# Seven block products in the experts' second layer as well, on a planned order of all engines, in a kernel of clustered attention and eight experts

## The chip, the cores and the metric

The kernel runs on one core of a Trainium2 chip. The metric is the device time of one execution in microseconds (us). TensorE is called PE here, VectorE DVE, ScalarE ACT, GpSimd POOL, and SyncE, which issues all DMAs, SP. "PEld" is the loading of a matmul's stationary operand.

## The reference, cut to what matters

```python
# attention: q, k, v are [4, 8, 768, 64]; a query sees the keys of its own cluster
scores = np.where(mask, scale * q @ k.T, -1e9); attn = softmax(scores); y = attn @ v
x = y.transpose(0, 2, 1, 3).reshape(3072, 512)
# experts: w_gate [512, 8], w1 [8, 512, 1024], w2 [8, 1024, 512]
P = exp(x @ w_gate - max)
for _ in range(8):                      # rows, then columns
    P /= P.sum(1, keepdims=True) + 1e-9; P /= P.sum(0, keepdims=True) + 1e-9; P *= N / E
for e in range(8):
    h = np.maximum(x @ w1[e], 0.0)      # first layer
    out += P[:, e:e + 1] * (h @ w2[e])  # second layer
```

All is float32.

## The kernel before, in words

**Attention.** The first stage works through 16 pairs of heads. A planner (`Planner`) sets its order: each step is a generator that yields an engine with a planned cost, and the planner records the instructions in the order of a planned time; `keep_order` makes each engine keep it. The result is x transposed, per batch of 768 tokens, stored in DRAM as `xd[b]`. `scan_first` finds expert 0's largest weights there, `first_x` makes the first batch's input tiles.

**Experts, first layer.** A number is held as two float16 parts, high and low, and a product is three matmuls: high by high, high by low, low by high. The tokens of a batch are split in two halves of 384, the 512 inputs in two halves, the features of a pair of 128-blocks in two: a 2x2 by 2x2 block product in seven products instead of eight (`layer1`). The seven operands from x (`XS`, with `LESS` for their differences) are made once per batch, the seven from the weights once per pair (`make_w`: four sums, then high and low parts). Each of the seven products is 6 matmuls (`product`, L1171), 128x128 stationary by 384 columns. Between them ACT scales a result out of PSUM (`scaled`, L1198) or DVE adds one (`add`, L1193); `relu_split` makes the high part with ReLU on ACT (L1182) and the low part on DVE (L1183). PSUM `h_ps` has two buffers.

**Experts, second layer.** It is a plain product (`layer2`): for each of 6 token blocks 6 matmuls of 512 columns (L1233 to L1235), summed in six PSUM banks over the four pairs of feature blocks. Once per batch and expert DVE takes the six results out, with the gate as factor, into `acc` (L1251, L1253).

I call one batch, one expert and one pair of feature blocks a **block**: 42 matmuls of 384 columns and 36 of 512. There are 4 x 8 x 4 = 128 blocks. Batches 0 and 1 take turns by expert through all eight experts, then batches 2 and 3.

**Weights.** In batch 0's turns `make_w` makes each pair's tiles `wa` (first layer) and `wb` (second layer, only split in high and low) and SP stores them in `wd`; every other batch loads them (`load_w`, 96 times). `scan` finds the next experts' largest weights. `gates` makes P, its 8 rounds crossing from DVE to PE and back.

**Order.** In this stage the code itself sets the order: the loop over `order` steps through generators (`making`, `scanning`, `inputs`, `sink`) between the seven products; layer 2 of a block runs between the products of the next one.

## Time and profile before

| What | Value |
|---|---|
| time, median of 3 runs | 2500.53 us (2497.03 to 2503.77) |
| profiled execution: span | 2493.7 us |
| its time around the span | not recorded apart; the median stands 6.8 us above the span |
| PE busy | 2390.6 us (96%), 12848 matmuls |
| DVE busy | 1372.4 us (55%) |
| ACT busy | 829.5 us (33%) |
| POOL busy | 669.5 us (27%) |
| first matmul of the first layer | 531.96 us after the span's start |
| last attention work on PE | 542.4 us |
| batches 2 and 3 | from about 1560 us to the end |

A row of a group reads: line, engine, operation, output<-inputs, shapes, count, then busy us, mean ns of one, then the engine's idle time just before them and what ended it. A row of a timeline reads: start us, duration us, engine, line, operation, count, and in brackets idle time and its releaser. A row of windows reads: stretch, its length, then busy us and count of PE, PEld, DVE, ACT and POOL, the granted share of the PE clock, the DMA engines' share and GB/s.

### The profile page before, as it was taken

The page shows a single profiled execution, that of the slowest core. Times are in us where ns is not written, and L with a number is a line of the kernel's source. Part 1 is how long each engine was busy: PE and PEld are TensorE (multiplying, and loading weights), DVE is VectorE, ACT ScalarE, POOL GpSimd, SP SyncE. Part 2 cuts the span into 40 slices and gives each one's busy share as a digit, 9 for nine tenths or more (in the row PEclk, how much of TensorE's full clock was granted, in tenths as well). Part 3 has the DMA queues.
Part 4 walks back from the last instruction along what each step waited for, and adds up shares of the span by engine and source line. Part 5 has one row for each costly group of instructions (what it writes and reads, how often), then busy time and mean ns, then how long its engine had stood idle before and what let it go on. Part 6 is the DMA issues. An engine that isn't in the chain of part 4 may idle for free.

```text
span 2493.7 us, 32865 instructions
## 1 busy us (share of the span) xinstructions
PE 2390.6 (96%) x12848; PEld 1281.1 (51%) x12848; DVE 1372.4 (55%) x2395; ACT 829.5 (33%) x1565; POOL 669.5 (27%) x683
## 2 busy tenths in 40 slices
...
DVE  7888787858755544444444446544443444444443
...
GB/s 165 139 120 121 124 99 112 97 144 232 237 277 255 147 158 108 146 124 130 135 141 113 125 47 138 103 113 96 93 101 108 94 94 109 101 93 94 114 103 89
DMA packets 154683, 320.30 MB, mean 128 GB/s; under 512 B 61088, under 2 KB 90528, under 8 KB 154016
## 3 DMA queue, kind: packets, MB, share of 16 engines
...
## 4 chain that ended last, share of the span: by engine, by line
PE 70%; DVE 8%; POOL 7%; DMA 7%; issue 6%; ACT 2%; SPq 0%; POOLq 0%; ACTq 0%; DVEq 0%
PE h_ps L1171 26%; PE o_ps L1233 10%; PE o_ps L1234 10%; PE o_ps L1235 10%; PE av_ps L817 4%; DMA r<-in_moe_w 3%; DMA scan<-in_moe_w 2%; POOL r L1091 2%; PE exp_ps L758 2%; PE max_ps L690 2%; PE exp_ps L759 2%; DVE mrt L694 2%; POOL wb L1100 1%; POOL wa L1103 1%; DVE am L286 1%
## 5 line engine op out<-in xcount | busy, mean ns | idle before, releaser
L1171 PEld LDWEIGHTS <-wa 128*128 128x128 f16 x5376 | 526.8, 98 | 478.5 <-issue 53.2
L1183 DVE SCALAR_TENSOR_TENSOR hl<-c,hh 128x384 f16<-128x384 f32 x512 | 313.6, 613 | 543.2 <-ACT hh L1182 542.7
L1171 PE MATMUL h_ps<-xsT,wa 128*128 128x384 f16 x3072 | 585.0, 327 | 13.8 <-ACT c L1198 6.9
L1233 PE MATMUL o_ps<-wb,hh 128*128 128x512 f16 x1536 | 584.5, 381 | 0.3 <-ACT hh L1182 0.3
L1234 PE MATMUL o_ps<-wb,hh 128*128 128x512 f16 x1536 | 583.9, 380 | 0.0
L1235 PE MATMUL o_ps<-wb,hl 128*128 128x512 f16 x1536 | 583.3, 380 | 0.7 <-DVE hl L1183 0.6
L1182 ACT ACTIVATE hh<-c 128x384 f16<-128x384 f32 x512 | 266.8, 521 | 853.4 <-DVE c L1193 848.5
L1171 PE MATMUL h_ps<-xsB,wa 128*128 128x384 f16 x2304 | 424.0, 328 | 25.1 <-DVE c L1193 20.9
L784 POOL TENSOR_TENSOR psum<-psum,pe 128x512 f32<-128x512 f32 (+1 forms) x216 | 231.4, 1088 | 57.3 <-ACT pe L765 50.1
L1235 PEld LDWEIGHTS <-hl 128*128 128x128 f16 x1536 | 151.0, 98 | 181.7 <-DVE hl L1183 2.9
L1193 DVE SCALAR_TENSOR_TENSOR c<-h_ps,u 128x384 f32<-128x384 f32 x256 | 142.0, 555 | 179.0 <-PE h_ps L1171 177.5
L1193 DVE SCALAR_TENSOR_TENSOR u<-h_ps,m 128x384 f32<-128x384 f32 x256 | 141.9, 554 | 163.7 <-PE h_ps L1171 163.7
L1233 PEld LDWEIGHTS <-hh 128*128 128x128 f16 x1536 | 150.8, 98 | 141.2 <-issue 1.7
L1234 PEld LDWEIGHTS <-hh 128*128 128x128 f16 x1536 | 150.7, 98 | 140.1 <-issue 1.6
L694 DVE TENSOR_REDUCE mrt<-max_ps 128x1 f32<-128x512 f32 (+1 forms) x288 | 190.5, 682 | 26.3 <-PE max_ps L690 24.1
L765 ACT ACTIVATE pe<-exp_ps 128x512 f32<-128x512 f32 x288 | 167.1, 597 | 111.4 <-PE exp_ps L759 96.2
L1198 ACT ACTIVATE c<-h_ps 128x384 f32<-128x384 f32 x128 | 62.5, 488 | 406.5 <-PE h_ps L1171 406.5
L1095 POOL TENSOR_TENSOR wa<-r,wa 128x256 f16<-128x256 f32 (+1 forms) x62 | 59.2, 972 | 344.6 <-ACT wa L1094 344.6
L1253 DVE SCALAR_TENSOR_TENSOR acc<-o_ps,gates,acc 128x512 f32<-128x512 f32 x168 | 125.3, 746 | 43.8 <-PE o_ps L1235 43.8
L690 PE MATMUL max_ps<-kX,qX 96*128 96x256 f32 (+1 forms) x384 | 127.2, 393 | 12.5 <-DVE mrt L694 11.7
L817 PE MATMUL av_ps<-pe,vn 128*64 128x512 f32 (+1 forms) x768 | 137.6, 501 | 0.0
L1091 POOL TENSOR_TENSOR r<-r 128x256 f32<-128x256 f32 x124 | 98.4, 814 | 116.1 <-ACT r L1081 113.7
...
## 6 DMA issues: line engine op xcount, KB each, us to landing
...
```

Source lines behind the costliest of these rows:

```text
L690: nc.tensor.matmul(ps[:, y * (z - a) : (y + 1) * (z - a)], t["qa"][0:96, i * P : (i + 1) * P], t["k2"][0:96, a:z], start=True, stop=True)
L694: nc.vector.tensor_reduce(out=t["mr"][:, i0 : i0 + ni, ni - 1], in_=ps.rearrange("p (x c) -> p x c", x=ni), axis=AX, op=ALU.max)
L765: nc.scalar.activation(pe, ps.rearrange("p (x c) -> p x c", x=ni), AF.Exp, scale=SCALE)
L784: (nc.gpsimd if e == POOL else nc.vector).tensor_tensor(out=st[:, a:z], in0=old[a], in1=part, op=ALU.add)
L817: nc.tensor.matmul(av[o, a:z], vn[:, i, :], heads[t]["pe", c][:, i - i0], start=(i == 0), stop=False, skip_group_check=True)
L1171: nc.tensor.matmul(ps[:, 0:HB], wa[:, w_, a, c, :], x[:, x_, c, :], start=(first and s_ == 0), stop=(s_ == len(steps) - 1), skip_group_che ...
L1182: nc.scalar.activation(hh[:, 2 - i, o], src, AF.Relu)
L1183: nc.vector.scalar_tensor_tensor(out=hl[:, 2 - i, o], in0=src, scalar=0.0, in1=hh[:, 2 - i, o], op0=ALU.max, op1=ALU.subtract)
L1193: nc.vector.scalar_tensor_tensor(out=t, in0=ps[:, 0:HB], scalar=KAPPA, in1=x, op0=ALU.mult, op1=ALU.add)
L1233: nc.tensor.matmul(po[i], hh[:, t, ti], wbh[:, t], start=(first and t == 0), stop=False)
L1234: nc.tensor.matmul(po[i], hh[:, t, ti], wbl[:, t], start=False, stop=False)
L1235: nc.tensor.matmul(po[i], hl[:, t, ti], wbh[:, t], start=False, stop=(last and t == 1))
```

## The change

**Second layer.** It is done in seven products too. Here the 2x2 blocks are the two token halves, the two feature blocks of a pair, and two halves of 256 output columns. The sums of h are made after ReLU on DVE (`relu_with`) and split like h itself (`split_raw`, `split_sum`); the sums of the weights are made once (`make_second`), split, and kept in DRAM (`wd2`). A **unit** is now one batch, one expert and two pairs of feature blocks: 84 matmuls of 384 columns and 7 x 3 x 6 = 126 of 256 columns. There are 64 units. `PIECES` lists the seven products, each in a part of two token blocks and a part of one. Their sums run in three PSUM banks (`a`, `c` and `ac`, which holds the third token block of both), and after each part DVE adds the running sum to `acc` with the gate (`collect`): 21 times per unit, 256 columns each. `BEFORE` says which `collect` a part waits for.

**First layer.** The same seven products in another order (`STEPS`), running through two `a` buffers and one `b` and one `c`; ACT scales four results out, DVE adds three.

**Order.** The whole stage is recorded by a second `Planner`; PE's order is written out in `run_pe` (one product of layer 1, then one part of layer 2 of the unit 18 products before), and the work of DVE, POOL, ACT and SP is put around it by planned costs. Sums and low parts go to POOL or DVE, as `either` chooses.

**Weights and batches.** From expert 1 on, batches 0 and 1 use a weight tile in turn before it is given up, so a tile is made or loaded once for the two; batches 2 and 3 do it from expert 0 (64 loads instead of 192). Expert 1 is scanned in the attention stage too. For batches 0 and 1, expert 0 is collected without a gate, and ACT applies the gate later.

```diff
-    LESS = {"T2": (("T1", "B12", "B11"), ("T2", "B22", "T1")), "B21": (("T4", "B21", "T2"), ("T3", "B22", "B12"))}
+    LESS = {
+        "T1": (("T1", "B12", "B11", "B11"), ("T3", "B22", "B12", "B12")),
+        "T2": (("T2", "B22", "T1", "T1"),),
+        "T4": (("T4", "B21", "T2", "B21"),),
+    }
...
-        def scan_first():
-            am8 = sm.tile([P, 2, NF], F32, name="am8", bufs=1)
+        def scan_first(e):
+            am8 = sm.tile([P, 2, NF], F32, name="am8")
...
+        for e in range(2):
+            plan.spawn(scan_first(e), urgency("values", nheads - 12 + 4 * e))
...
-    hp = ctx.enter_context(tc.tile_pool(name="hp", bufs=2))
-    ps_h = ctx.enter_context(tc.tile_pool(name="ps_h", bufs=2, space=PSUM))
-    ps_o = ctx.enter_context(tc.tile_pool(name="ps_o", bufs=6, space=PSUM))
...
+    rawp = ctx.enter_context(tc.tile_pool(name="rawp", bufs=4, **tiled))
+    sump = ctx.enter_context(tc.tile_pool(name="sump", bufs=2, **tiled))
+    cp = ctx.enter_context(tc.tile_pool(name="cp", bufs=2, **tiled))
+    wap = ctx.enter_context(tc.tile_pool(name="wap", bufs=4, **tiled))
+    NH = 20
+    hp = ctx.enter_context(tc.tile_pool(name="hp", bufs=NH, **tiled))
+    wbp = ctx.enter_context(tc.tile_pool(name="wbp", bufs=4, **tiled))
+    xp = ctx.enter_context(tc.tile_pool(name="xp", bufs=1, **tiled))
+    accp = ctx.enter_context(tc.tile_pool(name="accp", bufs=1, **tiled))
+    gs = ctx.enter_context(tc.tile_pool(name="gs", bufs=2, **tiled))
+    ps_a = ctx.enter_context(tc.tile_pool(name="ps_a", bufs=2, space=PSUM, **tiled))
+    ps_b = ctx.enter_context(tc.tile_pool(name="ps_b", bufs=1, space=PSUM, **tiled))
+    ps_c = ctx.enter_context(tc.tile_pool(name="ps_c", bufs=1, space=PSUM, **tiled))
+    ps_g = ctx.enter_context(tc.tile_pool(name="ps_g", bufs=1, space=PSUM, **tiled))
+    ps_2 = ctx.enter_context(tc.tile_pool(name="ps_2", bufs=1, space=PSUM, **tiled))
...
+    units = []
+    for c in range(B // 2):
+        for e in range(E):
+            turns = [(j, g) for g in range(NG2) for j in range(2)] if e else [(j, g) for j in range(2) for g in range(NG2)]
+            units += [(2 * c + j, e, g) for j, g in turns]
+    NU = len(units)
+    uses = {}
+    for u, (b, e, g) in enumerate(units):
+        uses.setdefault((b // 2, e, g), []).append(u)
...
+    ONE, TWO = 0.975, 0.982
+    SLOT = 14 * (ONE + TWO)
...
+    plan.PATIENCE = {"PE": 0.0, "ACT": 0.1, "POOL": 0.1, "SP": 0.1, "DVE": 0.1}
+    plan.free.update({PE: LEAD, ACT: 0.0, DVE: 0.0, POOL: 0.0, SP: 0.0})
...
+    def make_second(e, f2):
+
+        idx = e * NP2 + f2
+        s = uses[0, e, f2 // 2][0] + 1
+        need = piece_time(s, f2 % 2)
+        yield from after(s - 3)
+        yield ev["scale", e]
+        yield t_wb
+        yield t_raw
...
+        for o, a, b_, op in ((0, (0, 1), (0, 0), ALU.subtract), (1, None, (1, 1), ALU.subtract), (2, (1, 1), (0, 1), ALU.subtract), (3, (1, 0), None, ALU.add)):
+            w = yield either(0.82, 0.4)
...
+            by(w).tensor_tensor(out=T_[:, o], in0=x, in1=y, op=op)
...
+        t = wb[0, e, f2] = wbp.tile([P, 2, 7, MH], F16, name="wb")
+        for o, a, cost in ((slice(0, 1), Bk[:, 0, 0:1], 0.4), (slice(1, 3), Bk[:, 1], 0.61), (slice(3, 7), T_, 1.04)):
+            if cost > 0.4:
+                yield ACT, cost
+            nc.scalar.copy(t[:, 0, o], a)
+            w = yield either(2 * cost, 1.15 * cost)
+            by(w).tensor_tensor(out=t[:, 1, o], in0=a, in1=t[:, 0, o], op=ALU.subtract)
...
+        nc.sync.dma_start(out=wd2[idx], in_=t.rearrange("p x a m -> p (x a m)"))
...
+    STEPS = ((A11, "B11", "a"), (S1, "T1", "c"), (S2, "T2", "a"), (S4, "B22", "c"), (S3, "T3", "a"), (A12, "B21", "b"), (A22, "T4", "a"))
...
+        yield (t_a, t_c, ev["m1", k], ev["m5", k], ev["u2", k], t_b, ev["c22", k])[n]
+        yield PE, ONE
...
+    def scaled(t, ps, func=AF.Copy):
+        nc.scalar.activation(t, ps[:, 0:HB], func, scale=KAPPA)
+
+    def plus(t, ps):
+        nc.vector.scalar_tensor_tensor(out=t, in0=ps[:, 0:HB], scalar=KAPPA, in1=t, op0=ALU.mult, op1=ALU.add)
...
+    def split_raw(k, o, c):
+        yield t_h
+        yield ACT, 0.522
+        t = h[k, o] = hp.tile([P, 2, HB], F16, name="h")
+        nc.scalar.activation(t[:, 0], c, AF.Relu)
+        yield DVE, 0.607
+        nc.vector.scalar_tensor_tensor(out=t[:, 1], in0=c, scalar=0.0, in1=t[:, 0], op0=ALU.max, op1=ALU.subtract)
...
+    def split_sum(k, o, c):
+        yield t_h
+        yield ACT, 0.522
+        t = h[k, o] = hp.tile([P, 2, HB], F16, name="h")
+        nc.scalar.copy(t[:, 0], c)
+        w = yield either(0.95, 0.54)
+        by(w).tensor_tensor(out=t[:, 1], in0=c, in1=t[:, 0], op=ALU.subtract)
...
+            nc.vector.scalar_tensor_tensor(out=out_, in0=c, scalar=0.0, in1=other, op0=ALU.max, op1=op)
...
+        relu_with(s_1, c11, h21, ALU.add)
+        relu_with(h21, c22, h21, ALU.subtract)
+        relu_with(c22, c22, s_1, ALU.subtract)
+        relu_with(c12, c12, c22, ALU.add)
...
+    PIECES = (("A12", 1, "c", (1, 1)), ("A11", 0, "a", (1, 1)), ("S1", 3, "c", (2, 2)), ("S2", 4, "a", (1, 2)), ("S3", 5, "a", (2, 2)), ("A22", 6, "a", (2, 1)), ("S4", 2, "c", (1, 2)))
...
+    BEFORE = {
+        (0, 0): ((1, 6, 0),), (0, 1): ((1, 6, 1), (1, 5, 1)),
+        (1, 0): ((1, 5, 0),), (1, 1): ((0, 0, 1), (1, 5, 1)),
+        (2, 0): ((0, 0, 0),), (2, 1): ((0, 1, 1), (0, 0, 1)),
+        (3, 0): ((0, 1, 0),), (3, 1): ((0, 2, 1), (0, 1, 1)),
+        (4, 0): ((0, 3, 0),), (4, 1): ((0, 3, 1),),
+        (5, 0): ((0, 4, 0),), (5, 1): ((0, 4, 1),),
+        (6, 0): ((0, 2, 0),), (6, 1): ((0, 5, 1), (0, 2, 1)),
+    }
+    COLS = ((0, 1), (2,))
...
+        for d, m_, half_ in BEFORE[m, half]:
+            if u >= d:
+                yield ev["v", u - d, m_, half_]
+        yield PE, TWO * (4 if half == 0 else 2) / 3
+        opens = m in (0, 1) or (m == 2 and half == 0)
+        fresh = m < 3
+        for i in COLS[half]:
+            n = 0
+            for j in range(2):
+                t, w = h[(u, j), o], wb[b // 2, e, 2 * g + j]
+                for a_, b_ in ((0, 0), (0, 1), (1, 0)):
+                    nc.tensor.matmul(
+                        view(m, i), t[:, a_, i * P : (i + 1) * P], w[:, b_, x, :],
+                        start=(opens and n == 0 and i in (0, 2)), stop=(n == 5), skip_group_check=True,
+                    )
+                    n += 1
...
+            yield DVE, 0.37
...
+            if plain and first:
+                nc.vector.tensor_copy(to, src)
+            elif plain:
+                nc.vector.tensor_tensor(out=to, in0=src, in1=to, op=ALU.add)
...
+                nc.vector.scalar_tensor_tensor(
+                    out=to, in0=src, scalar=gate[b, e][:, ti : ti + 1], in1=to, op0=ALU.mult, op1=ALU.add
+                )
...
+    def run_pe():
+        ones_ = [(u, j, n) for u in range(NU) for j in range(2) for n in range(7)]
+        twos = [(u, m, half) for u in range(NU) for m in range(7) for half in range(2)]
+        for i in range(len(ones_) + 14 + LAG):
+            if i < len(ones_):
+                u, j, n = ones_[i]
+                if j == n == 0:
+                    ev["slot", u].set(plan)
+                yield from layer1(u, j, n)
+            if i >= 14 + LAG:
+                yield from layer2(*twos[i - 14 - LAG])
```

The first place is PE at the end of attention. Before, with `misc_ps` and `av_ps` of the last pair of heads and `h_ps` of the first layer:

```order
L817 MATMUL av_ps<-pe,vn 64x512 x4
L817 MATMUL av_ps<-pe,vn 64x256 x4
L825 MATMUL av_ps<-nht_206,ve 128x512
L825 MATMUL av_ps<-nht_206,ve 128x256
L854 MATMUL misc_ps<-psum,ones 32x384 x4
L1171 LDWEIGHTS wa
L1171 MATMUL h_ps<-xsB_5493,wa 128x384
```

In the changed kernel (`g_ps` is of the gates, `a_ps` of the first layer):

```order
L858 MATMUL misc_ps<-psum,ones 32x384 x4
L869 MATMUL misc_ps<-ident,sc 128x128 x3
L892 MATMUL misc_ps<-ident_r,rr 24x128
L903 MATMUL misc_ps<-rt,spread 128x128 x6
L934 MATMUL misc_ps<-xT,wg 32x256 x12
L946 MATMUL misc_ps<-ident,gt 128x96 x2
L1064 MATMUL g_ps<-ident,gmax 1x128
L1331 LDWEIGHTS wa
L1331 MATMUL a_ps<-xsB_5577,wa 128x384
```

The first layer stood between the steps of the last pair; now it stands behind all of them and behind the gates' first transpose.

The second place is POOL at the same point. Before, once the last sums of attention (`psum`) are done, it makes the next two pairs' weights, since DVE has made the first (`r` is the raw weight and its sums):

```order
L1091 TENSOR_TENSOR r_6163<-r_6163 128x256 x4
L1091 TENSOR_TENSOR r_6138<-r_6138 128x256 x3
L1095 TENSOR_TENSOR wa<-r_6138,wa 128x256
L1091 TENSOR_TENSOR r_6138<-r_6138 128x256
L1095 TENSOR_TENSOR wa<-r_6138,wa 128x512
L1103 TENSOR_TENSOR wa<-r_6138,wa 128x1024
L1100 TENSOR_TENSOR wb<-r_6140,wb 128x1024
L1095 TENSOR_TENSOR wa<-r_6163,wa 128x256
L1095 TENSOR_TENSOR wa<-r_6163,wa 128x512
L1100 TENSOR_TENSOR wb<-r_6165,wb 128x1024
L1103 TENSOR_TENSOR wa<-r_6163,wa 128x1024
```

In the changed kernel the first of all the sums stand between the last `psum` (`raw` and `sums` are the weights and their sums, `wa` and `wb` the low parts):

```order
L788 TENSOR_TENSOR psum<-psum,pe 128x256
L1162 TENSOR_TENSOR sums<-sums,raw 128x256
L788 TENSOR_TENSOR psum<-psum,pe 128x256
L1162 TENSOR_TENSOR sums<-raw 128x256
L788 TENSOR_TENSOR psum<-psum,pe 128x256
L1162 TENSOR_TENSOR sums<-raw 128x256
L1162 TENSOR_TENSOR sums<-sums,raw 128x256
L1170 TENSOR_TENSOR wa<-raw,wa 128x256
L1162 TENSOR_TENSOR sums<-raw,sums 128x256
L1170 TENSOR_TENSOR wa<-raw,wa 128x512
L1170 TENSOR_TENSOR wa<-sums,wa 128x1024
L1205 TENSOR_TENSOR sums<-raw 128x256
```

POOL now makes most of the first weights of both layers, beginning inside the tail of attention.

The third place is DVE in the middle of batches 0 and 1. Before (`u`, `c` are first-layer results, `hl` the low parts):

```order
L1193 SCALAR_TENSOR_TENSOR u_13341<-h_ps,m_13325 128x384
L1183 SCALAR_TENSOR_TENSOR hl<-c_13359,hh 128x384
L1193 SCALAR_TENSOR_TENSOR u_13379<-h_ps,m_13325 128x384
L1193 SCALAR_TENSOR_TENSOR c_13395<-h_ps,u_13379 128x384
L1183 SCALAR_TENSOR_TENSOR hl<-c_13395,hh 128x384
L1193 SCALAR_TENSOR_TENSOR c_13413<-h_ps,m_13325 128x384
L1183 SCALAR_TENSOR_TENSOR hl<-c_13413,hh 128x384
L1193 SCALAR_TENSOR_TENSOR c_13431<-h_ps,u_13341 128x384
L1183 SCALAR_TENSOR_TENSOR hl<-c_13431,hh 128x384
L1253 SCALAR_TENSOR_TENSOR acc_6827<-o_ps,gates,acc_6827 128x512
L1193 SCALAR_TENSOR_TENSOR u_13464<-h_ps,m_13448 128x384
```

In the changed kernel (`c`, `s`, `h_` numbers are results and sums of one pair, `h` the split parts, `acc` the collected sums):

```order
L1354 SCALAR_TENSOR_TENSOR c_11976<-b_ps,c_11976 128x384
L1558 SCALAR_TENSOR_TENSOR acc_7453<-ac_ps,gates,acc_7453 128x256
L1162 TENSOR_TENSOR sums<-raw 128x256
L1445 SCALAR_TENSOR_TENSOR s_12135<-c_11976,h_12129 128x384
L1558 SCALAR_TENSOR_TENSOR acc_7453<-a_ps,gates,acc_7453 128x256
L1362 SCALAR_TENSOR_TENSOR h<-c_11976,h 128x384
L1558 SCALAR_TENSOR_TENSOR acc_7453<-a_ps,gates,acc_7453 128x256
L1558 SCALAR_TENSOR_TENSOR acc_7453<-ac_ps,gates,acc_7453 128x256
L1445 SCALAR_TENSOR_TENSOR h_12129<-c_12000,h_12129 128x384
L286 TENSOR_REDUCE am_11240<-raw 128x1
L1445 SCALAR_TENSOR_TENSOR c_12000<-c_12000,s_12135 128x384
L1558 SCALAR_TENSOR_TENSOR acc_7559<-c_ps,gates,acc_7559 128x256
```

Collects of the second layer now stand between nearly all other instructions of DVE, with scans and weight sums among them.

659 lines of the change are left out of this document (401 added, 258 removed).

## The prediction

> **What bounds the kernel now.** I read the page first, then windows by stage, then timelines of the places that the change touches.
>
> ```profile
> span 2493.7 us, 32865 instructions
> PE 2390.6 (96%) x12848; PEld 1281.1 (51%) x12848; DVE 1372.4 (55%) x2395; ACT 829.5 (33%) x1565; POOL 669.5 (27%) x683
> DVE  7888787858755544444444446544443444444443
> ```
>
> PE is busy nearly throughout, but the share is a mean. (The third line is DVE's busy tenths in 40 slices; attention takes the first nine.) By stage (columns as in the note on windows above):
>
> ```profile
> 543.60:620.00 76.40, 57.06 (x259) 27.87 (x259) 59.63 (x127) 27.97 (x43) 30.61 (x25) 0.87 0.66 241
> 620.00:860.00 240.00, 218.38 (x1144) 111.73 (x1142) 154.34 (x241) 86.71 (x143) 81.20 (x72) 0.99 0.66 235
> 860.00:1560.00 700.00, 685.39 (x3645) 356.15 (x3644) 324.04 (x556) 233.24 (x401) 190.29 (x158) 1.00 0.36 124
> 1560.00:2494.00 934.00, 928.75 (x4959) 484.95 (x4956) 394.88 (x696) 192.97 (x386) 4.87 (x2) 1.00 0.28 100
> 1800.00:1900.00 100.00, 100.00 (x537) 52.29 (x536) 38.75 (x69) 20.72 (x42) 0.00 (x0) 1.00 0.27 95
> ```
>
> In batches 2 and 3 (from 1560) PE never rests: 537 matmuls in 100 us, so a block of 78 takes 14.5 us. In batches 0 and 1 it idles 19 us at the start, 22 up to 860, 15 after. DVE has half its time free, POOL three quarters or all. So the experts' stage is PE-bound; what the change does to PE's work counts in full, what it gives DVE and POOL counts once they fill up.
>
> ```profile
> 1700.01 1.14 PE L1171 MATMUL h_ps<-xsT,wa 128*128 128x384 f16 x6
> 1700.99 0.38 PE L1233 MATMUL o_ps<-wb,hh 128*128 128x512 f16 x1
> 1701.20 0.38 PE L1234 MATMUL o_ps<-wb,hh 128*128 128x512 f16 x1
> 1701.21 0.10 PEld L1235 LDWEIGHTS <-hl 128*128 128x128 f16 x1
> 1701.42 0.38 PE L1235 MATMUL o_ps<-wb,hl 128*128 128x512 f16 x1
> 66.00 0.34 PE L621 MATMUL misc_ps<-ident_b,om 128*128 128x128 bf16 x3
> ```
>
> A matmul's price is the distance of starts, not its duration. Six of 384 columns take 0.98 us, 0.1625 each; one of 512 takes 0.215.
>
> **PE's work.** Layer 1 keeps its 128 x 42 = 5376 matmuls: 5376 x 0.1625 = 873.6 us. Layer 2 had 4608 of 512 columns, 4608 x 0.2155 = 993.0 us. Now it has 64 x 126 = 8064 of 256 columns. No such row exists. Half of 0.2155 is 0.108; the line through 384 and 512 columns gives 0.2155 - 2 x 0.053 = 0.110. I take 0.109: 879 us, and 1753 us for both layers against 1867. The gain is **114 us**. It needs each matmul's own weight load (0.10 us) to fit under 0.109. That is close, but L621 issues three with a load each in 0.34 us, 0.06 apart after the first one's 0.22, so loads don't have to stand 0.10 apart. I charge nothing.
>
> **Where the stage begins.**
>
> ```profile
> 531.96 0.99 PE L1171 MATMUL h_ps<-xsB,wa 128*128 128x384 f16 x5
> 543.04 0.27 PE L1022 MATMUL h_ps<-ident,gmax 128*1 128x128 f32 x1 [0.69 <-DVE gmax L1019]
> 543.68 1.14 PE L1171 MATMUL h_ps<-xsT,wa 128*128 128x384 f16 x6 [0.37 <-DVE g L1024]
> 2488.89 0.38 PE L1235 MATMUL o_ps<-wb,hl 128*128 128x512 f16 x1
> ```
>
> Before, layer 1 fills gaps of attention's tail from 531.96. In the new order it stands behind L1064, the old L1022, so it starts at about **543.6**. In attention itself 16 more scans (half the width of L286 below, 0.6 us) lie on a DVE that has a fifth of its time free; I charge 0, at most 5.
>
> **The start-up.**
>
> ```profile
> L1091 POOL TENSOR_TENSOR r<-r 128x256 f32<-128x256 f32 x124 | 98.4, 814 | 116.1 <-ACT r L1081 113.7
> L1100 POOL TENSOR_TENSOR wb<-r,wb 128x1024 f16<-128x1024 f32 x31 | 66.7, 2152 | 128.0 <-ACT wb L1099 128.0
> L1095 POOL TENSOR_TENSOR wa<-r,wa 128x512 f16<-128x512 f32 x31 | 36.0, 1163 | 1.6 <-ACT wa L1094 1.6
> L1095 POOL TENSOR_TENSOR wa<-r,wa 128x256 f16<-128x256 f32 x31 | 24.2, 782 | 343.0 <-ACT wa L1094 343.0
> L296 POOL TENSOR_TENSOR tx<-xqB,tx 128x768 f32<-128x768 f32 x6 | 12.4, 2072 | 127.2 <-DVE xsT L303 63.7 <-issue 49.3 <-DMA xqB<-xd 14.1
> ```
>
> Up to the second `wb`, which layer 2 of the first unit needs, POOL's queue holds 16 sums (0.81), 3 + 4 + 5 low parts of 256, 512 and 1024 columns (0.78, 1.16, 2.15), 3 input sums (2.07), a split (384 columns, between the L1095 rows: 0.97) and three `psum`: about 41 us. It starts them near 531, so `wb` is there at 572 or, with waits for DVE, 576. PE is through the 18 products ahead of layer 2 at 543.6 + 18 x 0.975 = 561: 15 us of waiting. The fourth `wa` comes 15 us later still; I add 8 for it and 5 for the gates' crossings, which stand in PE's order: **28 us** (10 to 45).
>
> **DVE in batches 0 and 1.** This is the term I know least.
>
> ```profile
> L1193 DVE SCALAR_TENSOR_TENSOR c<-h_ps,u 128x384 f32<-128x384 f32 x256 | 142.0, 555 | 179.0 <-PE h_ps L1171 177.5
> L1253 DVE SCALAR_TENSOR_TENSOR acc<-o_ps,gates,acc 128x512 f32<-128x512 f32 x168 | 125.3, 746 | 43.8 <-PE o_ps L1235 43.8
> L904 DVE TENSOR_TENSOR xT<-misc_ps,xT 128x512 f32<-128x512 f32 x16 | 10.9, 684 | 9.7 <-PE misc_ps L899 9.6
> L904 DVE TENSOR_TENSOR xT<-misc_ps,xT 128x256 f32<-128x256 f32 x16 | 6.7, 417 | 4.8 <-PE misc_ps L899 4.7
> L286 DVE TENSOR_REDUCE am<-scan 128x1 f32<-128x1024 f32 x56 | 67.8, 1211 | 27.0 <-DMA scan<-in_moe_w 26.8
> L1183 DVE SCALAR_TENSOR_TENSOR hl<-c,hh 128x384 f16<-128x384 f32 x512 | 313.6, 613 | 543.2 <-ACT hh L1182 542.7
> L1183 DVE SCALAR_TENSOR_TENSOR hl<-c,hh x512: 495/558/1967, 539.7 to 2482.7; 128x384 f16<-128x384 f32 x171
> 2482.68 0.56 DVE L1183 SCALAR_TENSOR_TENSOR hl<-c,hh 128x384 f16<-128x384 f32 x1 [0.59 <-ACT hh L1182]
> 2483.16 0.74 DVE L1253 SCALAR_TENSOR_TENSOR acc<-o_ps,gates,acc 128x512 f32<-128x512 f32 x1
> ```
>
> A collect of 256 columns is L1253 less the difference of the two L904 rows: 0.746 - 0.267 = 0.48 us. Per unit: 21 x 0.48 = 10.1; 6 additions x 0.555 = 3.3; 6 low parts and 8 sums, x 0.558 = 7.8; 2 scans x 1.21 = 2.4; some 3 weight sums and splits 1.5; scales and gates 1: **26.1 us**. Two instructions that wait for nothing overlap: L1253 starts 0.48 after a start that lasts 0.56. Fifty overlaps of 0.08 make it 22.0. PE needs 84 x 0.1625 + 126 x 0.109 = 27.4 us per unit. So DVE just fits, were it alone. It isn't:
>
> ```profile
> 869.43 0.63 DVE L1183 SCALAR_TENSOR_TENSOR hl<-c,hh 128x384 f16<-128x384 f32 x1 [0.59 <-ACT hh L1182]
> 870.61 2.13 POOL L1100 TENSOR_TENSOR wb<-r,wb 128x1024 f16<-128x1024 f32 x1
> 871.62 1.54 DVE L1183 SCALAR_TENSOR_TENSOR hl<-c,hh 128x384 f16<-128x384 f32 x1 [1.09 <-ACT hh L1182]
> ```
>
> The second L1183 lasts 0.98 longer; it ends 0.42 after POOL's instruction does. DVE instructions with both inputs in SBUF stretch beside a busy POOL; L1193, which reads PSUM, doesn't. The new DVE has some 15.4 such of 384 columns per unit (6 + 8 + 1.4 splits). POOL's share per unit: 6.6 splits x 0.97, 6.2 sums x 0.81, 2 x 2.15, 1.6 x 1.16, 1.8 x 0.78 = 19 us, two thirds of the time. Lower bound of the stretch: L1183's mean over all is 0.613, 0.055 above its median, all from the half of them in batches 0 and 1, where POOL was busy a third: 0.11 each, 0.22 at two thirds, 3.4 us per unit. Upper: 0.98 x 2/3 x 15.4 = 10 us. I take the mean of the two rows above, (0.07 + 0.98) / 2 x 2/3 x 15.4 = 5.3, and for the bare work the middle, 24.1, as about half of the instructions follow a fresh result of ACT or PE. DVE then needs **29.5 us** per unit (25.4 to 36), 2.1 more than PE; over the 28 units after the start-up 28 x 2.1 = **59 us** (0 to 240).
>
> The Trainium skill says in "SBUF — State Buffer", Who interferes with whom, that a DVE instruction with two SBUF inputs contends with GpSimd's reads for one port pair held as an exclusive lock, the loser blocked for the whole instruction. By that, each such instruction waits on the mean 0.58 us whenever POOL is in one (the rest of instructions of the lengths above), 15.4 x 2/3 x 0.58 = 6.0 us per unit instead of 5.3, and the sum would be 20 us higher, an estimate. The row at 871.62 agrees with the lock.
>
> **The rest.** Batches 2 and 3: DVE has no scans and no weights, 21.7 us by durations, 18 overlapped; POOL makes 7 splits, 6.5 us, so 2 us of stretch. It fits under 27.4. What is late there is a collect: between a part and the next one that needs its bank PE has two products and a part of one block, 0.975 x 2 + 0.65 = 2.6 us, and two collects take 0.9, so DVE may be 1.7 late. I add 15 (before: 5 us idle there; 0 to 60). At the change of batches the inputs of batch 2 and then 3 put 14 us on DVE within one unit each: 2 x 7 = 15. ACT goes from 233 / 700 x 29.2 = 9.7 us per two blocks, by ten more instructions of 0.5 and the new weight sums' parts, to some 16.5 of 27.4: covered. DMAs halve in batches 2 and 3. Behind PE's last matmul come 4.8 us as before and about 1 of waits: 6.
>
> **Sum.** 543.6 + 1753 + 28 + 59 + 15 + 15 + 6 = 2420 us of span. The median stands 6.8 above the profiled span: 2427, 2.9% faster.
>
> **The rivals.** *DVE keeps up in batches 0 and 1 too* (T = 27.4 per unit): half of POOL's work falls where DVE reads PSUM. Without the 59 and some of the start-up: 2360. For it speaks the lower bound, 25.4; against it that DVE's order is fixed, so its idle moments aren't used. *DVE and POOL hold each other* in batches 0 and 1: at 33 us per unit (the full durations, 26.1, and 6.9 of stretch) the loss is 28 x 5.6 = 157 instead of 59, 2525, slower. It decides from 32 us per unit on (73 more over 28 units). By the Trainium skill's lock, as above, full durations would give 32.1, an estimate. Against it: the POOL row at 870.61 is not longer than its mean. *Collects come too late in all 64 units*: parts wait for banks throughout; 0.1 us on each of the 896 parts costs 75 more after what is charged, 2502, the same as before. *Loads don't hide under 256 columns*: at 0.12 per matmul 89 us more, 2516; L621 speaks against it.
>
> **Chances.** Forecast (DVE a little over PE in batches 0 and 1) 0.50; DVE keeps up 0.20; DVE and POOL hold each other 0.17, half of it slower; late collects 0.09, a third slower; loads 0.04. Faster than 0.3%, which is about what a measurement tells from no change, means below 2493: 0.83; within it 0.05; slower 0.12. The range reaches from the second case to the point where nothing is gained: 2355 to 2500. The likeliest alone has 2390 to 2465.
>
> **What would show it.** L1514, the new layer 2, starting 0.109 apart; first L1331 near 543.6 and PE idle 15 us before the first L1514; DVE above 90% and PE near 93% up to about 1510, PE at 99% behind it; L1445 and L1362 at 0.8 to 0.9 us in the first half, 0.57 to 0.65 in the second. I am wrong if PE idles in batches 2 and 3, if collects are far from 0.48, or if POOL's instructions stretch as DVE's do.

## The result, and the profile after

The changed kernel takes 2423.98 us (median of 4 runs, 2420.36 to 2426.88) against 2501.17 us in the same session (2497.03 to 2503.77): ratio 0.9695, 95% interval 0.9681 to 0.9709. It is 3.1% faster; 2427 was forecast. The total is right within 3 us, but several of its terms are not: five of them miss by 7 to 19 us each, and the misses cancel.

The page after, the lines that answer to those of before, with POOL's slices and the granted PE clock:

```profile
span 2423.0 us, 42921 instructions
PE 2296.8 (95%) x16304; PEld 1627.6 (67%) x16304; DVE 2064.0 (85%) x3818; ACT 1153.2 (48%) x2288; POOL 1278.1 (53%) x1257
...
DVE  7888878867998999999999999987777777777776
...
POOL 4776666677678667666766665432222322222221
PEclk6999999996899999999999999999999999999999
```

PE lost 94 us of busy time, DVE gained 692 and POOL 609. DVE's slices stand at 8 or 9 from the eleventh to the twenty-seventh: batches 0 and 1. The windows by stage (columns as before) show where PE rests:

```profile
557.95:642.50 84.55, 51.88 (x281) 31.27 (x280) 78.78 (x150) 42.34 (x72) 66.75 (x55) 0.74 0.36 127
...
697.30:1517.20 819.90, 785.88 (x5904) 579.63 (x5902) 778.72 (x1374) 449.73 (x850) 564.10 (x501) 0.99 0.38 130
1517.20:1630.30 113.10, 111.05 (x846) 82.36 (x844) 100.86 (x194) 48.92 (x96) 39.93 (x34) 1.00 0.27 88
1630.30:2423.00 792.70, 785.78 (x6044) 591.04 (x6041) 612.72 (x1220) 295.91 (x620) 208.81 (x200) 1.00 0.19 67
```

The bounds of the windows are starts of units: a unit is 84 matmuls of L1331, so every 84th one begins a unit. 697.30 is unit 4, 1517.20 unit 32, 1630.30 unit 36. In units 36 to 62 every unit takes 27.4 us, PE's own work, so nothing at all is lost there. In units 4 to 31 a unit takes 819.9 / 28 = 29.28 us. The start, units 0 and 1, is the first window: PE is busy 51.9 of 84.6 us, at a granted clock of 0.74.

Where layer 1 begins, and a group of 12 of the new layer 2's matmuls (timeline of PE):

```profile
557.78 0.37 PE L1064 MATMUL g_ps<-ident,gmax 128*1 128x128 f32 x1 [0.78 <-DVE gmax L1060]
557.95 1.81 PE L1331 MATMUL a_ps<-xsB,wa 128*128 128x384 f16 x5
...
884.40 1.47 PE L1514 MATMUL c_ps<-wb,h 128*128 128x256 f16 x12 [2.28 <-DVE acc L1558]
```

Twelve take 1.47 us, the last alone 0.27: (1.47 - 0.27) / 11 = 0.109 apart. DVE's groups in units 4 to 31, shapes kept apart:

```profile
L1362 DVE SCALAR_TENSOR_TENSOR h<-c,h 128x384 f16<-128x384 f32 x167 | 123.3, 743 | 2.4 <-ACT h L1360 2.4
L1558 DVE SCALAR_TENSOR_TENSOR acc<-a_ps,gates,acc 128x256 f32<-128x256 f32 x213 | 97.7, 474 | 15.9 <-PE a_ps L1514 15.8
...
L1445 DVE SCALAR_TENSOR_TENSOR c<-c,s 128x384 f32<-128x384 f32 x56 | 55.0, 982 | 0.4
L1445 DVE SCALAR_TENSOR_TENSOR s<-c,h 128x384 f32<-128x384 f32 x56 | 52.4, 937 | 0.0
```

and from unit 36 on, where POOL is busy 26% of the time instead of 69%:

```profile
L1558 DVE SCALAR_TENSOR_TENSOR acc<-a_ps,gates,acc 128x256 f32<-128x256 f32 x214 | 98.1, 479 | 56.5 <-PE a_ps L1514 54.7
...
L1362 DVE SCALAR_TENSOR_TENSOR h<-c,h 128x384 f16<-128x384 f32 x163 | 89.7, 550 | 5.4 <-ACT h L1360 5.4
```

The collect L1558, which reads PSUM, costs the same in both (0.474 and 0.479); L1362 and L1445, with both inputs in SBUF, stretch. POOL's low parts of 1024 columns stretch as well in units 4 to 31 (2.15 us before):

```profile
L1213 POOL TENSOR_TENSOR wb<-sums,wb 128x1024 f16<-128x1024 f32 x28 | 65.7, 2346 | 3.9 <-ACT wb L1211 3.5
```

Who ended PE's waits in units 4 to 31 (us in total, times, longest):

```profile
PE a_ps L1514 <- DVE acc L1558: 10.4, 13, 2.7
PE c_ps L1514 <- DVE acc L1558: 10.3, 7, 2.3
PE a_ps L1331 <- DVE c L1354: 3.9, 5, 1.0
```

The waits are few and long: 20 of them in 28 units, for a collect, make 20.7 us. This is what one looks like (timelines of POOL and DVE ahead of the PE row at 884.40 above):

```profile
879.31 2.45 POOL L1213 TENSOR_TENSOR wb<-sums,wb 128x1024 f16<-128x1024 f32 x1
...
880.08 1.96 DVE L1162 TENSOR_TENSOR sums<-raw 128x256 f32<-128x256 f32 x1
882.08 1.01 DVE L1162 TENSOR_TENSOR sums<-sums,raw 128x256 f32<-128x256 f32 x1
883.01 0.55 DVE L1371 TENSOR_TENSOR h<-c,h 128x384 f16<-128x384 f32 x1
883.48 0.86 DVE L1558 SCALAR_TENSOR_TENSOR acc<-c_ps,gates,acc 128x256 f32<-128x256 f32 x2
```

A weight sum of 256 columns, 0.42 us elsewhere, starts while POOL is in a low part of 1024 columns and ends 0.28 us after it: 1.96 us. Behind it in DVE's order stands the collect of the c bank. It ends at 884.34, and PE, which had waited 2.28 us for that bank, goes on at 884.40.

The 20 waits are alike. In 13 of them (15.8 us) one of the last six DVE instructions before the collect lasts over 1.3 us; in the other seven (4.9 us) one of the six is a scan of 1.2 us (L286). Only 110 of DVE's 1373 instructions in these units last 1.2 us or more. How long a hold is can be counted as well. Of the 391 instructions of L1362 and L1445 in these units, 217 start while POOL is in an instruction, and 215 of these end 0.41 to 0.49 us after POOL's does; their mean is 1.06 us. The other 174 take 0.55 us on the mean and 0.56 at most. The collects take 0.47 us in both cases.

### The profile page after: what moved, and what is told of

Its sections match the earlier page's. It is cut to its first block, busy times and chain, and to the rows that moved or that the text cites. A ratio compares the mean times of both kernels' runs of the same rounds, so it can differ in the third digit from the quotient of the medians.

```text
span 2423.0 us, 42921 instructions
## 1 busy us (share of the span) xinstructions
PE 2296.8 (95%) x16304; PEld 1627.6 (67%) x16304; DVE 2064.0 (85%) x3818; ACT 1153.2 (48%) x2288; POOL 1278.1 (53%) x1257
## 4 chain that ended last, share of the span: by engine, by line
PE 68%; DVE 25%; issue 3%; DMA 2%; ACT 1%; POOL 1%; SPq 1%; DVEq 0%; POOLq 0%; ACTq 0%
PE a_ps L1331 15%; PE a_ps L1514 11%; PE ac_ps L1514 9%; PE c_ps L1514 8%; PE c_ps L1331 7%; DVE acc L1558 5%; PE b_ps L1331 4%; PE av_ps L821 4%; DVE c L1445 3%; DVE h L1362 3%; PE max_ps L694 2%; DVE mrt L698 2%; PE exp_ps L762 2%; PE exp_ps L763 2%; DVE c L1354 1%
## 5 line engine op out<-in xcount | busy, mean ns | idle before, releaser
L1514 PEld LDWEIGHTS <-h 128*128 128x128 f16 x8064 | 791.3, 98 | 224.7 <-issue 40.2
L1331 PEld LDWEIGHTS <-wa 128*128 128x128 f16 x5376 | 528.9, 99 | 288.8 <-issue 37.8
L1360 ACT ACTIVATE h<-c 128x384 f16<-128x384 f32 x384 | 200.7, 523 | 537.4 <-DVE c L1354 536.8
L1331 PE MATMUL a_ps<-xsT,wa 128*128 128x384 f16 x2304 | 439.9, 327 | 13.8 <-ACT c L1351 7.0
L1514 PE MATMUL a_ps<-wb,h 128*128 128x256 f16 x3072 | 379.7, 274 | 12.9 <-DVE acc L1558 12.0
L1514 PE MATMUL ac_ps<-wb,h 128*128 128x256 f16 x2688 | 368.2, 273 | 2.4 <-DVE acc L1558 2.4
L1514 PE MATMUL c_ps<-wb,h 128*128 128x256 f16 x2304 | 284.9, 274 | 14.6 <-DVE acc L1558 11.9
L1558 DVE SCALAR_TENSOR_TENSOR acc<-a_ps,gates,acc 128x256 f32<-128x256 f32 x472 | 216.5, 477 | 83.2 <-PE a_ps L1514 81.1
L1362 DVE SCALAR_TENSOR_TENSOR h<-c,h 128x384 f16<-128x384 f32 x384 | 249.6, 652 | 8.6 <-ACT h L1360 8.6
L1371 POOL TENSOR_TENSOR h<-c,h 128x384 f16<-128x384 f32 x190 | 207.8, 1105 | 30.7 <-ACT h L1369 28.1
L1558 DVE SCALAR_TENSOR_TENSOR acc<-ac_ps,gates,acc 128x256 f32<-128x256 f32 x412 | 196.4, 477 | 32.2 <-PE ac_ps L1514 28.7
L698 DVE TENSOR_REDUCE mrt<-max_ps 128x1 f32<-128x512 f32 (+1 forms) x288 | 190.2, 682 | 38.9 <-PE max_ps L694 37.1
L1558 DVE SCALAR_TENSOR_TENSOR acc<-c_ps,gates,acc 128x256 f32<-128x256 f32 x352 | 155.4, 475 | 39.7 <-PE c_ps L1514 39.5
L1331 PE MATMUL c_ps<-xsB,wa 128*128 128x384 f16 x768 | 147.6, 329 | 11.7 <-ACT c L1351 11.7
L1331 PE MATMUL b_ps<-xsB,wa 128*128 128x384 f16 x768 | 148.6, 331 | 0.0
L1331 PE MATMUL a_ps<-xsB,wa 128*128 128x384 f16 x768 | 147.7, 329 | 0.0
L1331 PE MATMUL c_ps<-xsT,wa 128*128 128x384 f16 x768 | 146.9, 328 | 0.0
```

Source lines behind the costliest of these rows:

```text
L698: nc.vector.tensor_reduce(out=t["mr"][:, i0 : i0 + ni, ni - 1], in_=ps.rearrange("p (x c) -> p x c", x=ni), axis=AX, op=ALU.max)
L1331: nc.tensor.matmul(ps[:, 0:HB], wt[:, w_, a, c, :], xt[:, x_, c, :], start=(n in (0, 1, 5) and s_ == 0), stop=(s_ == len(steps) - 1), skip ...
L1360: nc.scalar.activation(t[:, 0], c, AF.Relu)
L1362: nc.vector.scalar_tensor_tensor(out=t[:, 1], in0=c, scalar=0.0, in1=t[:, 0], op0=ALU.max, op1=ALU.subtract)
L1371: by(w).tensor_tensor(out=t[:, 1], in0=c, in1=t[:, 0], op=ALU.subtract)
L1514: nc.tensor.matmul(view(m, i), t[:, a_, i * P : (i + 1) * P], w[:, b_, x, :], start=(opens and n == 0 and i in (0, 2)), stop=(n == 5), ski ...
```

## The experiments

**Why attention ends late.** Layer 1 starts at 557.95 instead of 543.6. The first run takes the second expert's scan out of attention again:

```
-        for e in range(2):
+        for e in range(1):
             plan.spawn(scan_first(e), ...)
...
-        if e > 1:
+        if e > 0:
             plan.spawn(scan(e), ...)
```

> Expert 1's scan goes back from attention into the experts' stage; nothing is left out. Theory A, the second scan in attention is what ends attention late (in the changed kernel the first L1331 starts at 557.95, 14.3 us behind the forecast): the first L1331 comes back to 544-548. In the stage 16 scans of 1.21 us then lie on a DVE that is full in units 0, 1 and 4 to 7, so between 0 and 19 us are given back: time 2410 to 2429 against 2424. Rival B, attention ends late for another reason (the new order of the inputs' sums in its tail): the first L1331 stays at 556-560 and the time goes up by 5 to 19 us.

(The text counts 16 scans of 1.21 us; 16 of 512 columns in attention are 8 of 1024 in the stage, 9.7 us.) Measured: 2427.38 us, ratio 0.9718 (0.9701 to 0.9735). Its first L1331:

```profile
540.91 1.81 PE L1331 MATMUL a_ps<-xsB,wa 128*128 128x384 f16 x5
```

17.0 us earlier: theory A, 3 us beyond its range. But unit 8 starts 3.5 us later than in the changed kernel (818.2 against 814.7), so 20.5 us were given back in the first eight units, twice the scans' 9.7 us on DVE. The times of the two kernels, 2427.38 and 2423.98, have ratios whose intervals overlap: having the scan in attention costs about as much as having it in the stage.

The second run leaves the order as it is and takes only DVE's time away:

```
-    largest(am8[:, m, f : f + 1], t)
+    largest(am8[:, m, f : f + 1], t if e == 0 else t[:, 0:32])
```

> The order of the changed kernel is kept, but expert 1's 16 scans in attention look at 32 of their 512 columns (about 0.1 us each instead of 0.6), so its scale is wrong by a factor. Theory A1, it is DVE's time in these scans that delays attention, 16 x 0.5 = 8 us: first L1331 at 549-551, time down by about 8 us. Rival A2, it is the place of the work in the fixed orders (the planner put attention in another order because of it), not DVE's time: first L1331 stays within 3 us of 558 and the time within 4 us of 2424.

Measured: 2418.62 us, ratio 0.9687 (0.9666 to 0.9708). Its first L1331:

```profile
548.92 1.48 PE L1331 MATMUL a_ps<-xsB,wa 128*128 128x384 f16 x4
```

9.0 us earlier, against 8 of DVE time removed: theory A1 by its number. But in two runs below (short scans, one reduction more), which do the same in the same order up to here as the changed kernel, the first L1331 stands at 555.16 and 553.81. The same attention thus ends up to 4 us apart, and 5 to 9 us of the 9.0 belong to the scans. The time is 5 us lower, not the expected 8, and the ratios' intervals overlap. The scans lie between 29 and 221 us (32 of L286, the median 0.67 us), far ahead of the tail. From there on the units are as long as before. The other 8 or so that the first run won come with attention's order, which the planner arranges anew when the scans go; which part of it was not tried.

**What paces the start-up.** PE's longest waits up to unit 2 of the changed kernel were these; `g_ps` is of the gates:

```profile
PE c_ps L1331 <- ACT c L1351: 10.8, 1, 10.8
PE g_ps L1092 <- DVE csum L1088: 8.2, 5, 7.3
PE g_ps L1070 <- DVE g L1067: 7.6, 1, 7.6
```

In the third run the gates start in the plan only behind the start of unit 1; in the fourth the work on batch 1's inputs does too.

```
     def gates():
+        yield ev["slot", 1]
         yield DVE, 0.3
```

> The gates' 8 iterations start only behind the start of unit 1 in the plan; nothing is left out. Theory C, DVE paces the start-up (it is busy from 557 to 642, with the gates' some 65 instructions, about 28 us, among the first weights): unit 2 starts 10 to 25 us earlier than 642.5 and, as later units take the gates' work on, the time falls by 5 to 20 us. Rival D, the first weights on POOL pace it (POOL has rows nearly without a gap from 559 to 633): unit 2 starts within 5 us of 642.5 less what the start of the stage moves, the time within 4 us of 2424 or above, since the gates' crossings then stand in the order of a PE that no longer waits.

> As the run before, and the scaling and splitting of batch 1's inputs (four maxima of 0.95 us, seven splits of 1.0 to 2.0 us on DVE, four sums of 2.1 us on POOL) also start only behind the start of unit 1. Theory C (DVE paces the start-up): unit 2 starts 20 to 35 us earlier than 642.5, some 10 us of it given back in units 2 to 4; time 2400 to 2412. Rival D (POOL's weights pace it): the four sums are 8 us of POOL, so unit 2 starts at most 8 us earlier and the time falls by at most 8.

Measured: 2413.78 us, ratio 0.9662 (0.9644 to 0.9680), and 2418.58 us, ratio 0.9686 (0.9668 to 0.9704). The windows up to unit 2 and from there to unit 4, of the one:

```profile
552.14:624.70 72.56, 48.76 (x275) 30.24 (x273) 65.24 (x114) 38.02 (x66) 57.62 (x46) 0.82 0.31 118
624.70:686.80 62.10, 59.69 (x428) 43.33 (x426) 56.45 (x120) 31.80 (x65) 34.01 (x34) 0.93 0.30 106
```

and of the other:

```profile
547.48:621.40 73.92, 55.33 (x310) 33.40 (x310) 59.16 (x111) 36.82 (x67) 56.51 (x51) 0.79 0.56 200
621.40:695.70 74.30, 61.33 (x430) 44.34 (x428) 65.39 (x144) 38.06 (x74) 39.79 (x36) 0.91 0.17 55
```

Without the gates unit 2 starts 17.8 us earlier and unit 4 10.5 us earlier. Of these, 5.8 us lie ahead of layer 1. There 1.1 are gained because the gates' first transpose no longer stands between attention's last matmul (L946) and the first L1331 (0.20 us apart instead of 1.31); the rest is attention itself ending earlier, and in the last two runs below, with the same late gates, it doesn't (first L1331 at 556.4 and 555.7). Counted from the first L1331, unit 2 starts 12.0 us earlier and unit 4 4.7. Rival D allowed 5 for unit 2, so this is theory C; the time falls by 10 us.

Without the inputs as well, unit 2 starts 21.1 us earlier, within the 20 to 35 expected, but 10.5 of these are the earlier first L1331, which in this order stands in attention's tail again. Unit 4 starts only 1.6 us earlier, since unit 2 takes 47.0 us instead of 27.4, and the time misses the expected 2400 to 2412. So the gates can wait, the inputs of batch 1, which unit 2 already needs, can't. What is left of the start-up's loss was not taken apart further; DVE is busy 65.2 of 72.6 us there.

**What paces units 4 to 31: amount, or the place of single holds.** Four runs in the changed kernel's order or near it. One takes DVE's work away (scans of 64 columns), one takes POOL's (its long low parts of `wa` and `wb` as ACT copies), one gives the planner the measured costs, one adds DVE work:

```
-            largest(am[:, m, f2 : f2 + 1], t)
+            largest(am[:, m, f2 : f2 + 1], t[:, 0:64])
```

> The order of the changed kernel is kept; the experts' stage's scans (48 of 1024 columns, experts 2 to 7, 1.2 us each on DVE) look at 64 of their columns, so the scales of those experts are off. POOL's and PE's work stays. Theory DVE, its time paces units 4 to 31 (29.28 us each on the mean against PE's 27.4): 1.7 scans x 1.1 us less per unit, so units 4 to 25 come to 27.4 to 28.2 and the time falls by 25 to 40 us. Rival POOL, the products wait for POOL's late h and weights and DVE is only busy, not late: units stay at 28.8 or more, the time falls by less than 10 us.

```
             w = yield either(2 * cost, 1.15 * cost)
-            by(w).tensor_tensor(out=t[:, 1, o], in0=a, in1=t[:, 0, o], op=ALU.subtract)
+            if w == POOL and cost > 0.5:
+                nc.scalar.copy(t[:, 1, o], a)
+            else:
+                by(w).tensor_tensor(out=t[:, 1, o], in0=a, in1=t[:, 0, o], op=ALU.subtract)
```

> The order of the changed kernel is kept; POOL's low parts of the weights of 512 and 1024 columns (two of each per unit, some 7 of POOL's 20.7 us per unit) are plain copies on ACT instead, so these low parts are wrong. DVE's instructions and their number stay. Theory stretch (a POOL in an instruction is what stretches DVE's two-SBUF-input instructions from 0.55 to 0.92-0.96 us, 3.9 us per unit now): a third less POOL takes 1.0 to 1.6 us of DVE's stretch from each unit, the mean of units 4 to 31 falls to 27.9-28.5 and the time by 22 to 40 us. Rival count (DVE's own durations fill it, the stretch falls where DVE would have waited): time within 8 us of 2424. Rival ACT: with 3.3 us more per unit (17.6 to 21) ACT comes late, time up.

```
-            yield DVE, 0.37
+            yield DVE, 0.475
...
-        yield DVE, 0.607
+        yield DVE, 0.80
...
-        yield DVE, 0.58
+        yield DVE, 0.80
...
-        w = yield either(0.95, 0.54)
+        w = yield either(0.95, 0.80)
...
-            w = yield either(0.82, 0.4)
+            w = yield either(0.82, 0.6)
...
-            w = yield either(2 * cost, 1.15 * cost)
+            w = yield either(2 * cost, 1.6 * cost)
```

> The planner is given DVE costs near those measured beside POOL (collect 0.475 for 0.37, two-input ones 0.80 for 0.54 to 0.61, weight sums 0.6 for 0.4, low parts by 1.6 for 1.15); it then gives every work that either engine may do to POOL. Nothing is left out. Theory DVE (amount): DVE loses some 3.5 instructions, 2 to 2.5 us, per unit, POOL takes 3 more (to 23.7 of 28): time down by 15 to 35 us. Rival POOL: DVE's remaining instructions meet a busier POOL (stretch from 3.9 to 4.7 us per unit) and second-layer products wait for h from POOL: time 2420 to 2445.

```
+        if n == 3 and j == 0 and u > 3:
+            plan.spawn(extra(u), lead + piece_time(u, 3))
...
+        x = gs.tile([P, 5], F32, name="extra")
+        nc.vector.tensor_reduce(out=x, in_=lg.rearrange("p t e -> p (t e)").unsqueeze(1).broadcast_to([P, 5, NTT * E]), axis=AX, op=ALU.max)
```

> One more DVE reduction of 960 columns (about 1.1 us) per unit in units 4 to 63, for which nobody waits. Theory DVE: it costs 0.6 to 1.1 us in each of units 4 to 31 (time up by 17 to 31 us) and nothing in units 35 to 62, which stay at 27.4 exactly, as DVE has 6 us free there. Rival, DVE is late at single places in all units rather than full (order, not amount): units 35 to 62 lengthen as well, by up to 0.5 us, and units 4 to 31 by less than 0.5.

Measured: 2411.98 us, ratio 0.9650 (0.9633 to 0.9668); 2369.30, 0.9478 (0.9464 to 0.9492); 2409.24, 0.9643 (0.9627 to 0.9658); 2436.20, 0.9751 (0.9735 to 0.9767). Windows over units 4 to 31, in the same order, a view of each kernel:

```profile
694.50:1504.10 809.60, 783.16 (x5903) 579.78 (x5901) 745.21 (x1374) 449.84 (x850) 569.49 (x501) 0.99 0.38 131
```

```profile
683.90:1460.80 776.90, 771.98 (x5904) 577.37 (x5902) 704.28 (x1374) 513.96 (x949) 371.02 (x402) 1.00 0.39 137
```

```profile
694.20:1494.50 800.30, 776.78 (x5903) 578.04 (x5901) 740.15 (x1280) 453.41 (x849) 643.78 (x596) 1.00 0.39 134
```

```profile
693.20:1526.30 833.10, 786.12 (x5903) 579.70 (x5901) 801.24 (x1403) 449.85 (x850) 563.47 (x500) 0.99 0.37 128
```

Per unit this is 28.91, 27.75, 28.58 and 29.75 us against 29.28. Summed durations (overlaps counted twice) say what each took from DVE, and the lengths of the 391 instructions of L1362 and L1445 (two SBUF inputs, 384 columns) say how they were held (means per unit and counts from the traces' rows):

| run | length of a unit | DVE durations | POOL durations | over 1.3 us, of 391 |
|---|---|---|---|---|
| changed kernel | 29.28 | 31.2 | 20.7 | 41 |
| short scans | 28.91 | 29.9 | 20.9 | 39 |
| long low parts on ACT | 27.75 | 28.2 | 13.6 | 2 |
| measured costs | 28.58 | 29.4 | 23.6 | 50 |
| one reduction more | 29.75 | 32.1 | 20.6 | 48 |

By **stretch** I mean what these 391 last beyond the 0.55 us that they take alone; in the changed kernel it is 3.9 us per unit.

Short scans: 1.4 us less of DVE per unit gains 0.37. Units at 27.4 to 28.2 were expected by the theory of amount; it falls. The rival's numbers fit better (28.8 or more; the time fell by 12 us, where it said less than 10), but not its reason, since PE's waits in this run are still the long ones for collects, and 1.0 us for POOL:

```profile
PE c_ps L1514 <- DVE acc L1558: 12.2, 7, 2.3
PE a_ps L1514 <- DVE acc L1558: 5.9, 9, 2.7
...
PE c_ps L1514 <- POOL wb L1213: 1.0, 1, 1.0
```

One reduction more, 1.14 us, costs 0.48 in units 4 to 31, less than the 0.6 expected at least, and nothing in units 36 to 62, which stay at 27.4: late collects throughout are excluded. The time rose by 12 us instead of 17 to 31. Neither of these two runs changes DVE's amount alone: a scan and this reduction are themselves single instructions of 1.1 to 1.2 us among the collects. Low parts on ACT: 3.0 us less of DVE durations, 2.3 of them stretch, gain 1.53, 43 of the 55 us that the run gained; the theory of stretch, above the 1.0 to 1.6 us of stretch and the 22 to 40 us expected. PE's waits there:

```profile
PE a_ps L1520 <- DVE acc L1564: 2.8, 3, 0.9
PE c_ps L1520 <- DVE acc L1564: 0.8, 1, 0.8
```

No wait is above 0.9 us. The measured costs move 3.4 instructions per unit from DVE to POOL; the stretch rises from 3.9 to 5.4 us per unit, and 0.70 us is gained all the same. The time falls by 15 us, the lower end of the 15 to 35 expected.

**Length or share.** The run on ACT took both POOL's share and its long instructions away. The next one takes only the length: the same low parts of `wa` and `wb` by POOL, in pieces of 256 columns. The order of the instructions on PE, DVE and ACT is the changed kernel's from first to last.

```
-            by(w).tensor_tensor(out=t[:, 1, o], in0=a, in1=t[:, 0, o], op=ALU.subtract)
+            for q in range(o.stop - o.start) if w == POOL else (slice(None),):
+                by(w).tensor_tensor(out=t[:, 1, o][:, q], in0=a[:, q], in1=t[:, 0, o][:, q], op=ALU.subtract)
```

> The order of the changed kernel is kept; POOL's low parts of 512 and 1024 columns (1.1 and 2.2 us each) are issued as two and four instructions of 256 columns (0.67 us each). Nothing is left out. POOL's busy time per unit goes up by 0.5 to 1.5 us (20.7 to 21-22), DVE's instructions stay. Theory length (a DVE instruction with two SBUF inputs is held until POOL's current instruction ends, so the long ones make DVE single instructions of 2 us, and collects behind these come late for their banks): the stretch per unit falls from 3.9 to 2.5-3.2 us, units 4 to 31 from 29.28 to 28.0-28.7 on the mean, the time by 15 to 35 us. Rival share (the stretch goes with POOL's busy share, whatever the lengths; the run that put these low parts on ACT gained by the share): stretch and units as before or longer, time 2420 to 2435.

Measured: 2384.92 us, ratio 0.9543 (0.9525 to 0.9560), 39 us faster than the changed kernel, 4 more than expected. Its window over units 4 to 31:

```profile
695.60:1478.80 783.20, 774.52 (x5904) 577.11 (x5903) 744.15 (x1373) 450.44 (x850) 625.93 (x709) 1.00 0.40 136
```

27.97 us per unit, although POOL is busy 625.93 us instead of 564.10 (by durations 23.2 us per unit instead of 20.7, more than the 0.5 to 1.5 expected). The groups of DVE and POOL that answer to L1445 `c<-c,s` and L1213 above, and PE's waits:

```profile
L1447 DVE SCALAR_TENSOR_TENSOR c<-c,s 128x384 f32<-128x384 f32 x56 | 43.7, 781 | 0.4
```

```profile
L1215 POOL TENSOR_TENSOR wb<-sums,wb 128x256 f16<-128x256 f32 x112 | 89.4, 827 | 1.7 <-ACT wb L1212 1.3
```

```profile
PE a_ps L1516 <- DVE acc L1560: 4.6, 8, 1.0
...
PE c_ps L1516 <- DVE acc L1560: 0.8, 1, 0.8
```

Of the 391 instructions 2 last over 1.3 us, where 41 did; their stretch falls from 3.9 to 2.9 us per unit. More of them than before start while POOL is in an instruction, 290 instead of 217, but these take 0.83 us on the mean instead of 1.06. PE's waits for collects on these two banks fall from 20.7 to 5.4 us. Theory length: the share of time beside POOL rose and the loss fell. The comparison with the short scans is the cleanest: both take 1.3 to 1.4 us of DVE durations from a unit, the scans gain 0.37 and the split 1.31, with a busier POOL. So it is for the most part not the amount but the long single hold in front of a collect that stops PE.

**Together.**

> The run before together with the measured DVE costs in the planner (that alone: 2409 us, POOL 23.6 us per unit, stretch 5.4). Nothing is left out. Theory length: the two add up, since one takes the long holds away and the other DVE's instructions: units 4 to 31 at 27.6 to 28.2, time 2375 to 2395. Rival: POOL with 25 us per unit is itself late with h: units at 28.5 or more, time 2405 to 2430.

Measured: 2384.80 us, ratio 0.9543 (0.9522 to 0.9564), the same as the split alone.

```profile
690.70:1473.60 782.90, 774.26 (x5904) 578.41 (x5902) 695.21 (x1280) 452.61 (x850) 690.75 (x809) 1.00 0.40 137
```

26 of the 28 units are at 27.4 to 28.2, 27.5 on the mean, but unit 5 takes 36.8 and unit 31 30.5 us: what the costs gain in the regular units they lose where expert 1's weights and batch 2's inputs come. Time and mean unit lie in the theory's range, but the two do not add up.

The last two put the split and the late gates together, with POOL's input sums of 768 columns halved; the second has the measured costs too.

```
-        by.tensor_tensor(out=t, in0=xq[a], in1=xq[c], op=ALU.subtract)
+        for k in range(KC) if by is nc.gpsimd else (slice(None),):
+            by.tensor_tensor(out=t[:, k], in0=xq[a][:, k], in1=xq[c][:, k], op=ALU.subtract)
```

> The split low parts (2385 us alone) with the gates behind unit 1's start (10 us faster alone), and POOL's sums of batch 1's to 3's inputs (768 columns, 2.1 us) issued as two of 384. Nothing is left out. Theory length: the parts add up, the 768-column sums hold DVE in units 0, 1 and 31 to 33 (where 4.6 us are lost at the change of batches): units 31 to 33 shorten by 1 to 3 us together, the start-up by 8 to 14: time 2368 to 2378. Rival: with the long holds gone the start-up is bound by the sum of DVE's work, which the gates' shift only moves on: 2380 to 2388.

> The run beside it with the measured DVE costs in the planner as well. Nothing is left out. Theory: units 8 to 30 at 27.4 as with both before, less DVE work in the start-up: 2362 to 2376. Rival: what the costs gain in units 8 to 31 they lose in units 5 and 31 to 33 (36.8 and 30 us with them, against 29.8 and 29 without), so no difference from the run beside it beyond 4 us.

Measured: 2372.24 us, ratio 0.9491 (0.9478 to 0.9504), and 2378.59 us, ratio 0.9513 (0.9500 to 0.9526). In the first, unit 4 starts at 684.0 (697.3 in the changed kernel), units 4 to 31 take 781.0 us, units 32 to 35 111.6 instead of 113.1, which they take with the split alone too: the three add up as expected (counted from the first L1331, units 0 to 3 take 127.6 us, with the split alone 139.6), and of the kernels that leave nothing out it is the fastest, 52 us ahead of the changed one and 127 of the one before. The second is 6 us slower, outside both what was expected (2362 to 2376) and the rival's 4 us; in its trace unit 5 takes 36.6 us again, as the rival said.

## Why the prediction was right in sum and wrong in parts

Units' starts give each term its measured size. PE's own work from the start of the stage to unit 4 is 18 x 0.975 + 38 x 1.957 = 91.9 us, a full unit 27.41 us.

| term | forecast | measured | from |
|---|---|---|---|
| start of the stage | 543.6 | 558.0 | first L1331 |
| both layers on PE | 1753 | 1754 | 64 x 27.41 |
| start-up, units 0 to 3 | 28 | 47 | 697.3 - 558.0 - 91.9 |
| DVE in units 4 to 31 | 59 | 52 | 819.9 - 767.5 |
| change of batches, units 32 to 35 | 15 | 3.5 | 113.1 - 109.6 |
| batches 2 and 3, units 36 to 63 | 15 | 0 | all at 27.4 |
| behind it | 6 | 7.5 | 2423.0 less the rest |

The measured sum is 3 us above the forecast of the span; the misses of 14 and 19 us upward meet 7, 11.5 and 15 downward. The median lies 1 us above the profiled span, where 6.8 were taken: the profiled execution itself took 2424.75 us, 1.8 more than its span, and the 6.8 set a span beside the median of other executions. That the total is right within 3 us is luck; the terms say how far the account holds.

**PE's work** was right. Starts 0.109 apart mean that each weight load hides under 256 columns, and of the gain of 114 us on PE 113 are there (1867 - 1754). A collect was forecast at 0.48 us and takes 0.474. Both came from differences of neighbouring rows; these were the terms with the best rows.

**Where the stage begins** failed in the sentence that charges the 16 scans in attention with 0, at most 5, since DVE has a fifth of its time free there. The run that shortens these scans begins layer 1 at 548.92, 5 to 9 us earlier for 8 us of DVE time: an engine's idle share says nothing of the places where its fixed order stands on the path. The size of this miss is uncertain: in the changed kernel's profile and those of the six runs from the short scans to the two edits together, which all leave attention's work as it is, layer 1 begins between 552.1 and 558.0, and 558.0 is the changed kernel's.

**The start-up** failed in its size. The forecast followed POOL's queue to the second `wb` at 572 to 576 and added 13 for the rest; that `wb` came at 596.5, the first L1514 at 610.40, and DVE was busy 78.8 of 84.6 us. The step left out DVE: the gates, charged 5 us as PE crossings, and batch 1's inputs lie in DVE's order among the first weights. PE waited 15.8 us for the gates' steps on DVE (the two `g_ps` rows above). Moving the gates alone brought unit 4 forward by 10.5 us, 4.7 of them behind the first L1331. It also left out that PE was granted less clock there: 0.74 up to unit 2. PE's own work up to there is 18 x 0.975 + 10 x 1.957 = 37.1 us, and it was busy 51.9; 4.6 of the difference are 21 matmuls of gates and scales, so some 10 of the 47 us went into slower matmuls.

**DVE in batches 0 and 1** has the right size, 29.28 for 29.5 us per unit, but the mechanism is only half right, so the size is in part luck. The stretch beside POOL is real: 14 instructions per unit at 0.834 us instead of 0.552 make 3.9 us, where 5.3 were taken for 15.4. But the forecast made it a sum, DVE's bare work plus stretch against PE's 27.4. DVE is busy 778.7 of 819.9 us, so it isn't full. Of the DVE time that the short scans take away a quarter is gained, of that which one more reduction adds under a half is lost; the split, which takes no more DVE time away than the short scans (1.3 us per unit), gained 36.7 of the 52 us. What stops PE is mostly a single hold of up to 2.6 us ahead of a collect. The Trainium skill states in "SBUF — State Buffer", Who interferes with whom, that a DVE instruction with two SBUF inputs contends with a GpSimd instruction that reads SBUF, for a port pair that is an exclusive lock; the page adds that whichever starts first has the pair for its whole instruction. By that the length of POOL's instructions matters, not its share alone. The row at 880.08, the 215 of 217 instructions that end just after POOL's, and the split's run agree with it. The prediction used that rule only for a mean of 6.0 us per unit, against 3.9 measured. The Trainium skill says in "Perfetto Trace Analysis", Optimizing Scalar/DVE Operations, of ScalarE and VectorE that breaking up instructions may help where they aren't saturated but make other engines wait. Here the instructions broken up were POOL's, which made PE wait by way of DVE; it gained 39 us. The Trainium skill says in the same section that moving work between GpSimd and VectorE might not help: the measured costs did so and gained 0.70 us per unit.

**Batches 2 and 3 and the change of batches** were charged with 15 us each, the one for collects that come late, the other for the inputs on DVE. Nothing is lost from unit 36 on, and 3.5 us at the change. POOL has only splits of 384 columns from unit 36 on, about 1 us each, and no DVE instruction lasts over 1.16 us, where a bank has 2.6 by the forecast; the reduction that was added there cost nothing either.

Of the rivals, loads that don't hide and collects late in all units are excluded by the same rows, and that DVE keeps up by the 52 us lost in units 4 to 31. "DVE and POOL hold each other" named the right partners with the wrong price: POOL's instructions stretch too (2.15 to 2.35 us, a sign that the prediction had put against itself), but a unit stays below the 32 us at which it would have decided.
